# A values block in the free columns of a scores bank, other prices for changes of TensorE's form, and new ranks

## The chip, the cores and the metric

The kernel runs on one NeuronCore of a Trainium2 chip. The metric is device time in microseconds (us) of one execution; lower is better. Engine names below are those of the profile: PE (TensorE), DVE (VectorE), ACT (ScalarE), POOL (GpSimd) and SP (the queue that issues nearly all DMAs).

## The reference: attention, then a token and a channel mixer

```python
def _attn_ref(q, k, v, n_global, n_local):       # (4, 8, 768, 64), float32; n_global 8, n_local 96
    scores = scale * np.matmul(q, k.transpose(0, 1, 3, 2))
    is_global = pos[None, :] < int(n_global)
    is_local = (rel >= 0) & (rel < int(n_local))
    keep = is_global | is_local
    dist = np.where(is_global & ~is_local, float(n_local), np.abs(rel))
    scores = scores + (-slopes[:, None, None] * dist)[None]
    scores = np.where(keep, scores, -1e9)
    a = np.exp(scores - np.max(scores, axis=-1, keepdims=True))
    return np.matmul(a / (np.sum(a, axis=-1, keepdims=True) + 1e-09), v)

def _moe_ref(x, w_tok1, w_tok2, w_ch1, w_ch2):   # x: (4, 768, 512)
    h = np.maximum(x.transpose(0, 2, 1) @ w_tok1, 0.0) @ w_tok2
    u = x + h.transpose(0, 2, 1)
    return u + np.maximum(u @ w_ch1, 0.0) @ w_ch2
```

A row of the scores keeps 96 local keys and 8 global ones. The four weights are float64 in the test's input and reach the kernel as their raw bits.

## The kernel before

**The work.** Attention is cut into 48 units v = 0 to 47, twelve to each of the four batches (`pair`, L536). A unit is two heads by 256 queries, or two by 192 where it starts a sequence. On PE a unit has up to three blocks: **S** (its scores, two PSUM banks), **T** (transposes of the weights, only for units 0 to 19; later units are turned by DMA transposes between `split` and `join`), and **V** (weights times values, two banks). Between S and V stand `max` on DVE (it reads the scores out of PSUM, once for each of the two banks), `exp` on ACT, `sum`, `inv`, `norm`, the turning, and `back` or `join`. `put` copies V's output out of PSUM. After the twelve units of a batch come the token mixer (**N** transposes, **J** and **U** products), then the channel mixer (**F** and **g** products of 12 and 6 matmuls, 48 steps k), and for the last two of its six chunks a form with fewer products (**P**, **G**, **H**). The weights are decoded on ACT, DVE and POOL into pairs of float32r tiles while the first batch's attention runs (`bits`, `down`, `shift`, `sign`, `high`, `low`).

**TensorE's two forms.** S and V blocks use 64x64 quarters of the array (`form="quarters"`), everything else the whole 128x128 array. PE changes form each time one kind follows the other.

**What sets the order.** `Plan` (L125 to 258) holds every piece of work with its engine, cost, predecessors, rank and what it takes and gives (tile slots by name; PSUM banks as tuples such as `("sp", v, e)`). `record` runs a list schedule over these costs: whenever an engine is free it takes, among the pieces whose predecessors have ended and whose slots and banks are free, the one of the lowest rank, and on PE adds a price for a change of form. The order of each engine's instructions in the program is the order in which the schedule started them; at run time nothing is reordered, and only semaphores make an engine wait. `fast` is built on the result, with ranks from long tables at L1250 ff. (`PAIRS` for units, `CHANNEL` for the steps k, `MIXES`, `PRI` and so on).

**Banks.** PSUM has eight banks of 512 columns (`self.banks`). A scores block fills at most columns 0 to 383 of its two, a values block at most columns 0 to 127. `bank` (L335) makes a tile of the whole bank, `[P, 512]`. The semaphores are set by the tile framework from the accesses to each tile: an access waits for the accesses to the same tile by other engines that were recorded before it.

Of the kernel before, what the change touches and what calls it, by code (L numbers as in the profile page):

```python
# [26 lines left out]
P = 128  # L27
# [103 lines left out]
class Plan:  # L131
# [7 lines left out]
    def __init__(self, room, busy, engines):  # L139
        self.room, self.busy, self.engines = dict(room), busy, engines  # L140
        self.work, self.order = {}, []

        self.banks, self.held = list(range(8)), {}

    def add(self, name, engine, cost, run, after=(), rank=0.0, take=(), give=(), form=None, move=None):

        costs = engine if isinstance(engine, dict) else {engine: cost}
        self.work[name] = dict(name=name, costs=costs, run=run, after=sorted(set(after)), rank=rank, take=take, give=give,  # L150
                               form=form, move=move, choice=isinstance(engine, dict))

    def record(self):
# [17 lines left out]
        while events:  # L171
# [3 lines left out]
            if what == "end":  # L175
# [9 lines left out]
                for g in w["give"]:  # L185
                    if isinstance(g, tuple):
                        banks.append(self.held[g])
                    else:
                        room[g] += 1
# [4 lines left out]
            for e, names in ready.items():  # L194
# [20 lines left out]
                for names in ready.values():  # L215
                    if n in names:
                        names.remove(n)
                for t in w["take"]:
                    if isinstance(t, tuple):
# [42 lines left out]
PORT = 0.05, 0.105  # L262

# [33 lines left out]
class Fast:  # L297
# [161 lines left out]
    def pair(self, v):  # L459
# [97 lines left out]
        def values():  # L557
# [6 lines left out]
            g["op"] = [self.bank("op", v, i) for i in range(2)]  # L564
# [33 lines left out]
        for e in range(2):  # L598
            add(f"max{v}{e}", "dve", 0.54 if j else 0.48, lambda e=e: maxima(e), [f"S{v}"] + ([f"max{v}0"] if e else []),
                r - PRI['max'], wp if e == 0 else [], [("sp", v, e)])  # L600
            add(f"exp{v}{e}", "act", 0.88 if j else 0.83, lambda e=e: exps(e), [f"max{v}{e}"], r - PRI['exp'])
        add(f"sum{v}", *(("pool", 0.32) if FIRST <= v < PER else ("dve", 0.19)), sums, [f"exp{v}0", f"exp{v}1"], r - PRI["sum"])
        add(f"inv{v}", "dve", 0.1, inverses, [f"sum{v}"], r - PRI["sum"])
        for e in range(2):
            for i in range(2):
                p = 0.4 if j else (0.34, 0.56)[i]
                add(f"norm{v}{e}" + "_0" * (1 - i), dict(dve=0.27, pool=p) if v < FIRST or PER - 3 <= v < PER else dict(pool=p),
                    0, lambda en, e=e, i=i: norm(e, i, en), [f"norm{v}{e}_0" if i else f"inv{v}"], r - PRI["norm"])
        if not far:
            add(f"T{v}", "pe", 0.7, transposes, [f"norm{v}0", f"norm{v}1"], r - PRI["T"],  # L610
                [("tp", v, 0), ("tp", v, 1)])
            for e in range(2):
                add(f"back{v}{e}", dict(act=0.37, dve=0.46), 0, lambda en, e=e: back(e, en), [f"T{v}"],
                    r - PRI["back"], (), [("tp", v, e)])
            late, give = "back", wp + (["w"] if FIRST <= v < PER else [])
        else:
            for e in range(2):
                add(f"split{v}{e}", "dve", 0.48, lambda e=e: split(e), [f"norm{v}{e}"] + ([f"split{v}0"] if e else []), r - PRI["split"],
                    [] if e else ["mix", "mix"])
                add(f"turn{v}{e}", "sp", 1.28, lambda e=e: turned(e), [f"split{v}{e}"], -1000, move=TURNED)  # L620
                add(f"join{v}{e}", dict(act=0.93, dve=0.5), 0, lambda en, e=e: join(e, en), [f"turn{v}{e}"], r - PRI["join"], (), ["p"])
            late, give = "join", ["mix", "mix"]
        add(f"V{v}", "pe", 0.68 if j else 0.63, values, [f"{late}{v}0", f"{late}{v}1"] + ([f"V{PER * b + n}"] if j else []), r - PRI["V"],
            [("op", v, 0), ("op", v, 1)] + (["w"] if v < H // 2 else ["x"] if b and j == 0 else []), give, "quarters")
        for i in range(2):
            add(f"put{v}{i}", dict(act=0.16, dve=0.2), 0, lambda en, i=i: put(i, en), [f"V{v}"], r - PRI["put"], (), [("op", v, i)])


    def tokens(self, b):
# [72 lines left out]
        for s in range(NS):  # L702

            done = range(4 * (s // 2), 4 * (s // 2) + 4) if b == 0 else range(PER)
            add(f"N{b}{s}", "pe", 0.36, lambda s=s: nat(s),
# [23 lines left out]
    def channel(self, q):  # L729
# [47 lines left out]
        for f in range(NF):  # L777
# [3 lines left out]
                r - PRI["F"], [("hp", k)])  # L781
# [448 lines left out]
GROUP = 0  # L1230

TURNS = 0.1, 0.15

TURN = 20000.0
# [6 lines left out]
def rank(kind, *at):  # L1241
# [8 lines left out]
WEIGHTS = [-247287.64, -257459.66, -159802.66, 108347.25, 701320.36, 727424.03, 731700.59, -176028.47, -459899.46,  # L1250
    748998.43, -38407.14, 719519.09, -9340.29, 41643.28, 649601.75, -293679.97, -289307.55, -286192.76, -286154.59,
    599029.48, -288533.39, 576521.07, 574350.69, 619086.99, 690632.99, 615663.67, 350737.42, 602403.1, 350663.18,
    316597.46]
LOADS = [613978.2, 312816.36, 625641.67, 661111.23, 634176.56, 421225.21, 779927.82, 261887.11, 364054.34,
    634156.02, 779954.04, 379228.08, 364081.73, 749680.16, 379239.78, 3198492.43, 944262.45, 693856.62, 942541.96,
    944250.08, 364126.34, 262402.44, 3214978.83, 341772.37, 450658.52, 209511.38, 198960.32, 261800.84, 198940.7,
    3134618.01]
CHANNEL = [301486.65, 143282.3, 182530.41, 140462.62, 301502.01, 301530.53, -445928.27, 234721.3, -528799.29,
# [5 lines left out]
PAIRS = [-1226940.92, -1226961.87, -41406.37, -1244067.5, -73629.74, -39713.61, -3405.65, -570391.63, 16314.72,  # L1264
# [5 lines left out]
PRI = {'q': -136472.84, 'max': 36946.91, 'exp': 564950.24, 'sum': 384246.62, 'norm': -75198.73, 'T': 377235.02,  # L1270
    'back': -67350.38, 'split': -146960.38, 'join': 586267.28, 'V': 171989.17, 'put': 204986.15, 'F': -599619.09,
    'mix': 1187119.78, 'hid': 282479.97, 'send': 35006.69, 'high': 307017.91}
PRI2 = {'early': 38778.45, 'quad': -995662.53, 'mixed': -322415.37, 'second': -162956.33, 'step': -65687.24,
    'zmixed': 432393.84, 'hid': -315881.55, 'half': -273398.98, 'less': 233896.24, 'lstep': -298323.36, 'lstep2':
    -767970.86, 'late': -656740.22, 'evac': 433382.65, 'other': 235872.85}
OPERANDS = [-266472.19, -132411.79, -126401.41, 250209.8, 250863.15]
FORMS = [-101606.63, 339654.31, 605149.18, -102559.01, 567856.28, 867487.13, -122475.58, 490959.25, -205979.65,
    -96045.46, 547370.76, 423744.95]
PARK = [529904.06, -94029.49, 431875.51, 430818.8]
UNPARK = [464099.4, 464058.48]  # L1280
MIXES = [[211216.27, 227215.94, 235324.42, -655468.27, 276409.17, 413038.91, 275470.81, -587105.86, -579070.2,
# [255 lines left out]
```

## Time and profile before

| | |
|---|---|
| times of 3 runs | 579.27, 577.6, 579.19 us (median 579.19) |
| profiled execution | 577.9 us, its span 576.0 us |
| granted TensorE clock | 0.998 |
| PE busy | 558.8 us, 97% of the span |
| DVE, ACT, POOL busy | 413.0 (72%), 311.0 (54%), 291.0 us (51%) |
| PE's share of the chain that ended last | 85% |

The span runs from the first to the last instruction of the profiled execution; 1.9 us of its time lie around it. PE is busy nearly throughout, but over the first 56 us the slices of the profile's picture of busy time show it at 60 to 90%, and DVE and ACT at 80 to over 90%.

### The profile page before, as it was taken

Reading aid. Unit: us, or ns where it says so; the run is one execution under the profiler, and the core shown is the slowest. Engines: PE = TensorE matmul, PEld = TensorE weight load, DVE = VectorE, ACT = ScalarE, POOL = GpSimd, SP = SyncE. Lnnn points to the kernel's source line nnn. Section 1 sums busy time; section 2 is a strip of 40 time slices with the busy share of each in tenths; the row PEclk is TensorE's granted clock in tenths of the full one; section 3 lists DMA queues with packets and bytes.
Section 4 is the critical chain, followed back from the end, with each engine's and each line's share of the span. In section 5 each row is a group of like instructions: output and inputs, shape, how many; then the busy total and the mean of one; then the engine's idle time right before and its main releaser. Section 6 shows DMA issues by size and latency. Waiting matters only on the chain.

```text
span 576.0 us, 12239 instructions
## 1 busy us (share of the span) xinstructions
PE 558.8 (97%) x4402; PEld 454.5 (79%) x4402; DVE 413.0 (72%) x1029; ACT 311.0 (54%) x800; POOL 291.0 (51%) x405
## 2 busy tenths in 40 slices
PE   6889999999999999999999999999999999999996
PEld 5657887788888888888887887787788878888885
DVE  4998999976678888566436877657635964449885
ACT  3999988876645666333433723543533533337340
POOL 3796678531128777153305697714200233139982
PEclk9999999999999999999999999999999999999999
DMA  7948692877212879957320447998402173445013
GB/s 258 395 151 307 226 349 78 250 205 263 73 38 75 193 229 266 376 116 216 87 81 2 127 184 160 328 335 166 97 6 75 55 238 109 152 141 183 0 39 114
DMA packets 72083, 97.08 MB, mean 169 GB/s; under 512 B 47952, under 2 KB 51152, under 8 KB 72016
## 3 DMA queue, kind: packets, MB, share of 16 engines
q1 hardware_dynamic: 71728, 96.09, 53.7%
q8 instruction: 37, 0.61, 0.4%
q14 instruction: 30, 0.25, 0.1%
q10 hardware_dynamic: 288, 0.13, 0.1%
HBM read 63.18 MB, written 22.02 MB: 148 GB/s over the span
## 4 chain that ended last, share of the span: by engine, by line
PE 85%; DVE 4%; DMA 3%; ACT 3%; POOL 3%; issue 1%; ACTq 1%; SPq 0%; POOLq 0%
PE hp L288 31%; PE acc L288 22%; PE last L288 10%; PE pu L288 5%; PE op L288 5%; PE pj L288 5%; PE sp L288 4%; DVE pp L288 2%; DMA p<-r 2%; PE xtp L288 2%; PE tp L288 1%; DMA w<-wc 1%; POOL pp L288 1%; ACT pp L288 1%; DVE r L288 1%
## 5 line engine op out<-in xcount | busy, mean ns | idle before, releaser
L288 PE MATMUL hp<-uh,wc 128*128 128x512 f32 x432 | 140.9, 393 | 0.3 <-PE sp L288 0.3
L288 PE MATMUL acc<-hh,wc 128*128 128x512 f32 x384 | 120.7, 395 | 0.0
L288 POOL TENSOR_SCALAR p<-p,st 128x192 f32<-128x192 f32 (+1 forms) x132 | 80.2, 624 | 56.2 <-ACT p L288 30.6
L288 PEld LDWEIGHTS hp<-uh,wc 128*128 128x128 f32 x432 | 81.1, 188 | 20.1 <-ACT u L288 1.2
L288 PE MATMUL hp<-ul,wc 128*128 128x512 f32 x216 | 84.2, 390 | 0.0
L288 PEld LDWEIGHTS acc<-hh,wc 128*128 128x128 f32 x384 | 70.5, 188 | 16.4 <-issue 1.7
L288 PE MATMUL acc<-hl,wc 128*128 128x512 f32 x192 | 74.9, 390 | 0.0
L288 DVE COPY r<-p 128x768 uint16<-128x768 uint16 x82 | 54.1, 680 | 21.8 <-DMA p<-r 14.0
L288 ACT ACTIVATE p<-p,st 128x192 f32<-128x192 f32 (+1 forms) x132 | 57.4, 439 | 16.8 <-DVE st L288 16.8
L288 ACT ACTIVATE hh<-hp 128x512 fp32r<-128x512 f32 x48 | 28.6, 595 | 58.5 <-PE hp L288 38.4
L288 POOL TENSOR_TENSOR o<-uh,ul 128x512 f32<-128x512 f32 x16 | 22.8, 1435 | 66.1 <-DVE t L288 37.3
L288 DVE SCALAR_TENSOR_TENSOR hl<-hp,hh 128x512 fp32r<-128x512 f32 x48 | 33.0, 687 | 23.6 <-ACT hh L288 23.4
L288 DVE SCALAR_TENSOR_TENSOR t<-w,t 128x512 int32<-128x512 int32 x60 | 43.5, 729 | 6.1 <-ACT w L288 3.5
L288 PEld LDWEIGHTS hp<-ul,wc 128*128 128x128 f32 x216 | 40.6, 188 | 8.0
L288 POOL TENSOR_SCALAR e<-e,sc 128x256 f32<-128x256 f32 x37 | 24.1, 654 | 43.3 <-DMA e<-pk 31.2
L288 ACT COPY r<-p 128x768 uint16<-128x768 uint16 x30 | 31.6, 1066 | 21.6 <-DMA p<-r 12.4
L288 PEld LDWEIGHTS acc<-hl,wc 128*128 128x128 f32 x192 | 36.0, 188 | 7.7
L288 DVE CUSTOM_DVE_ANT_0 p<-sp,bias 128x192 f32<-128x192 f32 (+1 forms) x132 | 37.7, 343 | 5.3 <-PE sp L288 5.2
L288 POOL TENSOR_TENSOR hid<-hid 128x512 f32<-128x512 f32 x14 | 19.8, 1412 | 36.5 <-ACT hid L288 35.7
L288 PE MATMUL sp<-e 64*64 64x192 f32 (+1 forms) x624 | 32.4, 329 | 1.3 <-ACT e L288 0.8
L288 DVE TENSOR_TENSOR lent<-lent 128x256 f32<-128x256 f32 (+1 forms) x48 | 31.2, 683 | 1.9 <-ACT lent L288 1.8
L288 POOL TENSOR_SCALAR pp<-pp,st 128x192 f32<-128x192 f32 (+1 forms) x50 | 23.1, 476 | 10.2 <-DVE st L288 9.1
(184 smaller groups left out, 1196.8 us busy)
## 6 DMA issues: line engine op xcount, KB each, us to landing
e<-pk SPq DMA_DIRECT2D x24, 592.0 KB, 5.5
w<-wc SPq DMA_DIRECT2D x24, 512.0 KB, 6.7
sd<-lent SPq DMA_DIRECT2D x24, 512.0 KB, 3.5
e<-pk SPq DMA_DIRECT2D x14, 560.0 KB, 5.1
back<-wd SPq DMA_DIRECT2D x8, 768.0 KB, 7.3
lent<-sd SPq DMA_DIRECT2D x10, 512.0 KB, 3.8
sm<-sd SPq DMA_DIRECT2D x16, 256.0 KB, 3.3
unit<-pk SPq DMA_DIRECT2D x9, 384.0 KB, 6.4
```

The lines of the kernel that those rows point to most:

```text
L288: ins = getattr(self.engine, name)(*args, **kw)
```

## The change

- A pair of banks can hold one S block and one V block at a time. `join` puts a block into the latest pair that has none of its kind (`shared`), or takes two fresh banks; `leave` gives a bank back when both of its blocks are done with it. V writes columns 384 to 511 of its banks instead of 0 to 127; S stays where it was. In `bank` both blocks of a pair get **the same tile object**, so a shared bank goes by one name (that of the block that came first: an output `sp` of a V block, or `op` of an S block).
- The plan's price for a change of form goes from 0.1 and 0.15 us to 0.2 and 0.25 us in its time, its weight in the choice (`TURN`) from 20000 to 1209.99, and `GROUP`, which favours quarters when more of them are ready, from 0 to 20.92. `N` costs 0.44 us instead of 0.36.
- Four tables are added that shift the ranks of single units or steps (`SOFT`, `VALUES`, `PUTS`, `FIRSTS`), and all other ranks are new. The arithmetic is the same.

```diff
+    def shared(self, tokens):
+        if tokens[0][0] not in SLOTS:
+            return None
+        return next((p for p in reversed(self.pairs) if tokens[0][0] not in p["use"]), None)
+    def join(self, tokens):
+        p = self.shared(tokens)
+        if p is None:
+            p = dict(use=set(), banks=[self.banks.pop(0) for _ in tokens], left=[0, 0], tiles={})
+            self.pairs.append(p)
+        p["use"].add(tokens[0][0])
+        for t in tokens:
+            self.owner[t] = p
+            p["left"][t[2]] += 1
+    def leave(self, token):
+        p, e = self.owner[token], token[2]
+        p["left"][e] -= 1
+        if not p["left"][e]:
+            self.banks.append(p["banks"][e])
+            self.pairs = [x for x in self.pairs if x is not p]
...
-                    if len(some) <= len(banks) and all(room[t] >= w["take"].count(t) for t in w["take"] if t not in some):
+                    if (len(some) <= len(banks) or self.shared(some)) and all(room[t] >= w["take"].count(t) for t in w["take"] if t not in some):
...
+SLOTS = "sp", "op"
...
-        i = self.plan.held[(name, *key)]
-        return self.ps.tile([P, 512], F32, tag=f"b{i}", name=name)
+        pair = self.plan.owner.get((name, *key))
+        if pair is None:
+            i = self.plan.held[(name, *key)]
+            return self.ps.tile([P, 512], F32, tag=f"b{i}", name=name)
+        e = key[-1]
+        if e not in pair["tiles"]:
+            pair["tiles"][e] = self.ps.tile([P, 512], F32, tag=f"b{pair['banks'][e]}", name=name)
+        return pair["tiles"][e]
...
-            g["op"] = [self.bank("op", v, i) for i in range(2)]
+            g["op"] = [self.bank("op", v, i)[:, 384:] for i in range(2)]
...
-                r - PRI['max'], wp if e == 0 else [], [("sp", v, e)])
+                r - PRI['max'] + SOFT[v], wp if e == 0 else [], [("sp", v, e)])
...
-GROUP = 0
-TURNS = 0.1, 0.15
-TURN = 20000.0
+GROUP = 20.92
+TURNS = 0.2, 0.25
+TURN = 1209.99
...
+VALUES = [-648691.61, 62020.51, -661316.06, -60827.32, -467294.93, -879603.85, -879479.46, -66299.9, -373273.58,
...
```

Counted over the whole program, PE has 46 unbroken groups of quarter blocks before and 37 now; 12 of them stand ahead of the first J product in both. 26 of the V blocks share their banks with an S block. From the last J products of the fourth batch on, some 140 us before the end, all engines' orders are the same. Ahead of the first U product of the first batch PE had S of unit 21, T of unit 16 and V of units 16 and 17, which now stand behind it; nothing has come in their place.

Three places of the order follow. The first is DVE in the softmax of the first units, from the copy that completes unit 0's transposed weights (`back`), with what each row waits for. The two rows of `ISA` are the `max` of unit 1, one for each bank, the copies are unit 0's `put`, the last row is the first `max` of unit 3. Before, DVE has there:

```order
L288 COPY pp<-tp 128x384 [waits PE_49]
L288 ISA pp,st<-sp,bias 128x2x64 [waits PE_49]
...
L288 ISA pp,st<-sp,bias 128x2x64 [waits PE_49]
...
L288 COPY x<-op 128x128 [waits PE_49] x2
L288 ISA pp,st<-sp,bias 128x2x64 [waits PE_49]
```

Now DVE has there, with the shared bank under the name `sp`:

```order
L321 COPY pp<-tp 128x384 [waits PE_49]
L321 ISA pp,st<-sp,bias 128x2x64 [waits PE_49]
...
L321 ISA pp,st<-sp,bias 128x2x64 [waits PE_49]
...
L321 COPY x<-sp 128x128 x2
L321 ISA pp,st<-sp,bias 128x2x64 [waits PE_49]
```

The rows stand in the same order, but V of unit 0 now lies in the bank of unit 1's scores, and the copies out of it wait for nothing: the `max` rows ahead of them already wait for V's last matmul into that bank.

The second is PE a little later: V of unit 1 (`e_59` holds its values), with waits. Before, PE has there:

```order
L288 MATMUL op<-pp,e_59 64x128 [waits DVE_49]
L288 MATMUL op<-pp,e_59 64x128 [waits Activation_49]
L288 MATMUL op<-pp,e_59 64x128 [waits PE_49]
L288 MATMUL op<-pp,e_59 64x128 x3
L288 MATMUL op<-pp,e_59 64x64 x6
```

Now PE has there, again with the scores' bank as output:

```order
L321 MATMUL sp<-pp,e_59 64x128 [waits DVE_49]
L321 MATMUL sp<-pp,e_59 64x128 x5
L321 MATMUL sp<-pp,e_59 64x64 x6
```

Before, V waits for the two copies that bring its weights, one on DVE and one on ACT. Now it lies in the bank of unit 5's scores, and the one wait on DVE is for the last `max` of unit 5, which stands behind both copies on DVE.

The third is PE at the end of the fourth batch's attention (units 44 to 47; `e_58` to `e_61` hold a unit's loaded q, k and v; a row `64x192` is an S block, `64x128` with `64x64` a V block). Before, it is S and V blocks of 47 between those of 44 and 46:

```order
L288 MATMUL op<-r,e_58 64x128 x8
L288 MATMUL op<-r,e_58 64x64 x8
L288 MATMUL sp<-e_61 64x192 x8
L288 MATMUL op<-r,e_60 64x128 x8
L288 MATMUL op<-r,e_60 64x64 x8
```

Now the last group that holds an S block on PE is this one:

```order
L321 MATMUL sp<-e_60 64x192 x8
L321 MATMUL sp<-r,e_58 64x128 x8
L321 MATMUL sp<-r,e_58 64x64 x8
L321 MATMUL op<-r,e_61 64x128 x8
L321 MATMUL op<-r,e_61 64x64 x8
```

S of unit 46 has moved behind the products g of steps 42 and 43 and is now the last S block. V of unit 44 lies in its bank. Behind this group stand F of steps 44 and 45 and g of step 44, then V of units 45 and 46; before, S of unit 46 stood ahead of the second half of g of step 41, and the last S block was 47's.

## Rows read from the trace of the kernel before

**Rows 1.** The page: busy time of PE, and the chain that ended last.

```profile
PE 558.8 (97%) x4402; PEld 454.5 (79%) x4402; DVE 413.0 (72%) x1029; ACT 311.0 (54%) x800; POOL 291.0 (51%) x405
...
PE 85%; DVE 4%; DMA 3%; ACT 3%; POOL 3%; issue 1%; ACTq 1%; SPq 0%; POOLq 0%
```

**Rows 2.** Busy time by stretch: length, then PE, PEld, DVE, ACT, POOL; clock, DMA.

```profile
14.00:28.00 14.00, 12.42 (x252) 9.18 (x244) 13.14 (x82) 13.89 (x60) 10.49 (x30) 1.00 1.04 400
...
42.00:56.00 14.00, 12.72 (x281) 10.66 (x280) 11.65 (x47) 13.37 (x45) 9.67 (x17) 1.00 0.80 291
56.00:77.48 21.48, 21.36 (x317) 17.26 (x316) 20.97 (x56) 19.68 (x54) 14.14 (x23) 1.00 0.70 251
77.48:130.00 52.52, 52.52 (x425) 42.27 (x420) 46.46 (x118) 43.93 (x103) 32.11 (x33) 1.00 0.70 208
```

**Rows 3.** PE's timeline around a group of four quarter blocks: start, us, instructions.

```profile
255.31 0.39 PE L288 MATMUL acc<-hl,wc 128*128 128x512 f32 x1
255.63 0.88 PE L288 MATMUL sp<-e 64*64 64x192 f32 x16
256.33 0.85 PE L288 MATMUL op<-r,e 64*64 64x128 f32 x32
256.99 0.83 PE L288 MATMUL sp<-e 64*64 64x192 f32 x16
...
258.42 0.50 PE L288 MATMUL hp<-uh,wc 128*128 128x512 f32 x1
258.76 0.39 PE L288 MATMUL hp<-ul,wc 128*128 128x512 f32 x1
258.99 0.40 PE L288 MATMUL hp<-uh,wc 128*128 128x512 f32 x1
```

**Rows 4.** Timeline of PE, DVE and ACT in the first softmaxes.

```profile
13.78 0.29 DVE L288 CUSTOM_DVE_ANT_0 pp<-sp,bias 128x128 f32<-128x128 f32 x1 [0.73 <-PE sp L288]
...
14.45 0.22 PE L288 MATMUL op<-pp,e 64*64 64x64 f32 x1
...
19.16 0.76 PE L288 MATMUL op<-pp,e 64*64 64x128 f32 x18
...
19.92 0.82 PE L288 MATMUL sp<-keys,unit 64*64 64x192 f32 x14
...
20.39 0.08 DVE L288 DVE_READ_ACCUMULATOR2_ANT st<- 128x1 f32 x1
...
20.79 0.36 DVE L288 CUSTOM_DVE_ANT_0 pp<-sp,bias 128x192 f32<-128x192 f32 x1 [0.32 <-PE sp L288]
...
21.08 0.35 DVE L288 CUSTOM_DVE_ANT_0 pp<-sp,bias 128x192 f32<-128x192 f32 x1
...
22.43 0.46 ACT L288 ACTIVATE pp<-pp,st 128x192 f32<-128x192 f32 x1
```

**Rows 5.** Groups of ACT instructions from 12 to 76 us: busy us, mean ns.

```profile
L288 ACT COPY pp<-tp 128x384 f32<-128x384 f32 x15 | 7.0, 491 | 2.2 <-PE tp L288 2.2
...
L288 ACT ACTIVATE w<-w 128x512 f32<-128x512 f32 x8 | 5.5, 690 | 0.1
...
L288 ACT COPY x<-op 128x128 f32<-128x128 f32 x18 | 4.5, 293 | 0.3 <-PE op L288 0.2
...
L288 ACT CAST wc<-t 128x512 fp32r<-128x512 f32 x2 | 1.2, 622 | 0.7 <-DVE t L288 0.7
...
L288 ACT ACTIVATE unit<-unit,sc 128x256 f32<-128x256 f32 x1 | 0.5, 492 | 0.0
```

**Rows 6.** Timeline in the fourth batch: V of unit 37, S and last join of 47.

```profile
361.28 0.72 PE L288 MATMUL op<-r,e 64*64 64x128 f32 x16 [0.85 <-ACT r L288]
...
408.18 0.83 PE L288 MATMUL sp<-e 64*64 64x192 f32 x16
...
418.71 1.07 ACT L288 COPY r<-p 128x768 uint16<-128x768 uint16 x1
```

**Rows 7.** The page's DMA issues: the loads of a unit, KB, median us to landing.

```profile
e<-pk SPq DMA_DIRECT2D x24, 592.0 KB, 5.5
```

More of the change, by code (lines that the diff above doesn't have):

```diff
@@ L217, in record @@
                         names.remove(n)
+                some = [t for t in w["take"] if isinstance(t, tuple)]
+                if some and some[0][0] in SLOTS:
+                    self.join(some)
                 for t in w["take"]:
+                    if t in self.owner:
+                        continue
                     if isinstance(t, tuple):
@@ L599, in pair @@
             add(f"max{v}{e}", "dve", 0.54 if j else 0.48, lambda e=e: maxima(e), [f"S{v}"] + ([f"max{v}0"] if e else []),
-                r - PRI['max'], wp if e == 0 else [], [("sp", v, e)])
-            add(f"exp{v}{e}", "act", 0.88 if j else 0.83, lambda e=e: exps(e), [f"max{v}{e}"], r - PRI['exp'])
-        add(f"sum{v}", *(("pool", 0.32) if FIRST <= v < PER else ("dve", 0.19)), sums, [f"exp{v}0", f"exp{v}1"], r - PRI["sum"])
-        add(f"inv{v}", "dve", 0.1, inverses, [f"sum{v}"], r - PRI["sum"])
+                r - PRI['max'] + SOFT[v], wp if e == 0 else [], [("sp", v, e)])
+            add(f"exp{v}{e}", "act", 0.88 if j else 0.83, lambda e=e: exps(e), [f"max{v}{e}"], r - PRI['exp'] + SOFT[v])
+        add(f"sum{v}", *(("pool", 0.32) if FIRST <= v < PER else ("dve", 0.19)), sums, [f"exp{v}0", f"exp{v}1"], r - PRI["sum"] + SOFT[v])
+        add(f"inv{v}", "dve", 0.1, inverses, [f"sum{v}"], r - PRI["sum"] + SOFT[v])
         for e in range(2):
@@ L613, in pair @@
                 add(f"back{v}{e}", dict(act=0.37, dve=0.46), 0, lambda en, e=e: back(e, en), [f"T{v}"],
-                    r - PRI["back"], (), [("tp", v, e)])
+                    r - PRI["back"] + SOFT[v], (), [("tp", v, e)])
             late, give = "back", wp + (["w"] if FIRST <= v < PER else [])
@@ L704, in tokens @@
             done = range(4 * (s // 2), 4 * (s // 2) + 4) if b == 0 else range(PER)
-            add(f"N{b}{s}", "pe", 0.36, lambda s=s: nat(s),
+            add(f"N{b}{s}", "pe", 0.44, lambda s=s: nat(s),
                 [f"put{PER * b + v}{i}" for v in done for i in range(2)] + ([f"N{b}{s - 1}"] if s else []), r[s], [("xtp", b, s)])
@@ L1258 @@
-CHANNEL = [301486.65, 143282.3, 182530.41, 140462.62, 301502.01, 301530.53, -445928.27, 234721.3, -528799.29,
[5 rows of a table removed]
-PAIRS = [-1226940.92, -1226961.87, -41406.37, -1244067.5, -73629.74, -39713.61, -3405.65, -570391.63, 16314.72,
[5 rows of a table removed]
-PRI = {'q': -136472.84, 'max': 36946.91, 'exp': 564950.24, 'sum': 384246.62, 'norm': -75198.73, 'T': 377235.02,
-    'back': -67350.38, 'split': -146960.38, 'join': 586267.28, 'V': 171989.17, 'put': 204986.15, 'F': -599619.09,
-    'mix': 1187119.78, 'hid': 282479.97, 'send': 35006.69, 'high': 307017.91}
@@ L1273 @@
[L1273 to L1278, printed above, removed]
@@ new lines @@
+CHANNEL = [-2949169.64, -2510927.96, -3101480.77, -3123168.36, 576525.89, -2949169.27, -2947017.06, 955741.29,
[5 rows of a table added]
+PAIRS = [18126.21, -2488994.4, -75805.74, -191767.69, -142830.03, -2578991.51, -127250.42, -2457092.07, -126917.67,
[5 rows of a table added]
+PRI = {'q': -549637.56, 'max': 477943.31, 'exp': 1141466.61, 'sum': 881334.09, 'norm': 8677.43, 'T': 1141636.88,
+    'back': -188132.18, 'split': 60902.38, 'join': -528669.37, 'V': 277212.65, 'put': -528612.38, 'F': -545988.49,
+    'mix': 2305531.53, 'hid': 1665439.57, 'send': -356818.58, 'high': -259803.05}
@@ new lines @@
+PRI2 = {'early': -615955.21, 'quad': -726503.67, 'mixed': -600476.22, 'second': -241800.96, 'step': -625074.95,
+    'zmixed': -241788.36, 'hid': -656604.26, 'half': -326301.11, 'less': -241766.64, 'lstep': -414355.74, 'lstep2':
+    -884616.08, 'late': -864145.14, 'evac': -881205.61, 'other': -682843.25}
+OPERANDS = [-252627.04, -159434.83, -158488.82, -60757.83, -43455.52]
+FORMS = [1446332.6, 1432096.45, 1409418.05, 1423655.59, -119437.76, -116408.75, -286337.7, -119095.62, -94850.63,
+    -119433.56, -110237.18, -136161.96]
@@ L1288, in fast @@
+PARK = [65986.45, 64471.52, 19323.32, -648759.28]
+UNPARK = [-292592.4, 45309.19]
+MIXES = [[-912803.0, 384130.46, 270996.01, -912780.48, -683115.09, -655544.44, -798870.1, -569781.86, 320263.84,
[5 rows of a table added]
 @with_exitstack
```

39 lines of the change are left out of this document (21 added, 18 removed), and 49 rows, old and new, of tables (CHANNEL, FIRSTS, MIXES, PAIRS).

## The prediction

> **What bounds the kernel now.** I read the page first, then busy time by stretch, then the timeline at the places that the change touches. PE is busy for 558.8 of 576.0 us and has 85% of the chain that ended last [rows 1]. So the end is PE's start plus its work plus its idle time, and the change leaves the work alone. The stretches show where PE can wait. From 77.48 us, the start of the first U product, to 130 it is busy for 52.52 of 52.52 us. Before that, ACT is what is full: 13.89 of 14 us from 14 to 28, 13.37 of 14 from 42 to 56, with DVE at 13.14 and 11.65 and PE at 12.42 and 12.72 [rows 2]. So up to 77 us the pace is ACT's and DVE's, and PE idles between; after it, PE's own instructions count one for one. A saving on PE is worth its full price behind 77.48 us and little ahead of it.
>
> **The change of form.** The group of four quarter blocks at 255.63 gives its price. Two full matmuls follow each other by 258.99 - 258.76 = 0.23 us; from the last full one to the first quarter it is 255.63 - 255.31 = 0.32, so going in costs 0.09. A quarter block takes 256.99 - 256.33 = 0.66; the four take 258.42 - 255.63 = 2.79, or 0.15 more than 4 x 0.66. The first full matmul after them takes 0.34 instead of 0.23: another 0.11 [rows 3]. A trip into quarters and back costs 0.35 us. There were 46 and are 37. The 9 that go stand behind the first J product; 3 of them stand ahead of 77.48 us, 6 behind it. Behind: 6 x 0.35 = **-2.1 us**, in full. The 3 ahead of it (1.05 us) only let PE wait longer, if ACT and DVE still set the pace there.
>
> **The shared banks.** This is the part that the plan has no price for. A shared pair is one tile, so `max` of the S block waits for the V block in the same bank where V was recorded first, and V waits for `max` where that was first. The trace of before has no such case, since S and V never lay in one bank; its cost is bounded from both sides: nothing, where the later one would have come later anyway, and at most the whole of the other's work. Three cases lie early, where ACT is full.
> - Unit 1's first `max` starts at 13.78 now. V of unit 0 has its last matmul at 14.45 and ends at 14.67 [rows 4]. `max` moves behind it: 0.9 later, and with it the `exp` for which ACT stands idle there.
> - V of unit 1 starts at 19.16 and S of unit 6 is behind it on PE (19.92), whose `max` is at 20.79. Unit 5's last `max` ends at 20.39 + 0.08 = 20.47. V of unit 1 has to wait for that, itself 0.9 later: 21.37. Then S of unit 6 0.76 later at 22.13 and its `max` 0.87 after that at 23.0; its `exp`, at 22.43 now [rows 4], can start when the first half of `max` is through, some 0.3 later: 23.3. So here too ACT is **0.9 us late** in all (the first delay is in it). DVE's two `put` copies now stand between and wait for the same V.
> - Two `put` of unit 3 on ACT lie in the bank of unit 7's scores, ahead of unit 7's `exp`, and wait for both its `max`. `exp` could start after the first; the second comes two reductions later, 2 x (21.08 - 20.79) = **0.6 us** [rows 4].
>
> Is ACT's list ahead of the first U product shorter? At the `exp` of unit 6 it has left out two `back` and two `put` that it had done by then, 2 x 0.49 + 2 x 0.29 = 1.6 us. Up to the last J product's relu the new list has one `exp` less (two of 0.46, 0.9), six `put` less (1.8), one `high` less (0.6), but two `q` and one `down` more (1.0 + 0.7): 1.6 us less in all [rows 4, 5]. The two cancel, so the lateness of 1.5 us stays and the first U product starts **1.5 us later**, unless ACT's remaining idle time takes it up: 0.11 + 0.63 us in the two stretches shown and 1.8 from 56 to 77.48 [rows 2].
>
> **What PE has not done by then.** S of unit 21, T of unit 16 and V of units 16 and 17 now stand behind the first U product. At 0.66 us a block [rows 3] that is 4 x 0.66 = **+2.6 us** of work that PE did in its idle time and now does where it has none.
>
> **Late waits.** V of unit 37 waited 0.85 us for its join [rows 6]; two more F blocks now stand ahead of it: -0.85. At the end of the fourth batch, S of unit 47 started at 408.18 and its last join ended at 418.71 + 1.07 = 419.78, 11.6 us later [rows 6]. The last S is now unit 46's, with V of 44 in its bank, so its `max` waits 0.66 more: 12.3. PE has behind it V of 44 and 47, F of 44 and 45, g of 44 and V of 45: with S itself 4 x 0.66 and 36 matmuls of 0.23, and one trip, 2.6 + 8.3 + 0.35 = 11.2 us. V of 46 waits **1.1 us**, and N is behind it. S of 45 and 46 need loads that V of 41 and 42 release; a load lands after 5.5 us [rows 7] and `q` takes 0.5 [rows 5], 6.0 and some 0.3 for two semaphores, against 24 matmuls of 0.23 and a trip, 5.9: 0.3 each, **0.6**. In all +0.85.
>
> **The sum.** -2.1 + 1.5 + 2.6 + 0.85 = +2.9 us, against the execution's own 577.9: 580.8. That execution is 1.3 under the median of the three runs; two of the four times lie near 577.7 and two near 579.2, so I add half of it, 0.6: **581.4 us**.
>
> The Trainium skill, in PSUM — Partial Sum Buffer, section PSUM bank collisions raise a hardware error, says that engines must be kept apart by bank and group of 32 partitions, not by address: a V block in other columns of the bank that `max` reads would still collide. No run here shows such a pair. If engines could be let into one bank in different columns, the waits of 0.9, 0.6 and 0.66 would go, and by the sum above the time would be 2.2 us less, 579.2.
>
> **Rivals.**
> - *The trips come through in full and the early lateness is taken up.* For it: ACT has 2.5 us of idle time in the stretches named. Then the first U product comes earlier by as much as PE's list is shorter, and what is left is 9 x 0.35 = -3.15: 574.8, or 575.4 by the runs. Against it: DVE and ACT cannot run ahead of their lists, and these are no shorter where it counts.
> - *Early lateness is taken up in part, late waits stay out.* The first U product starts when it did or a little sooner (-1), +2.6 - 2.1 and half the late waits: 0 on balance, 578.5.
> - *Bank guards pile up.* 26 V blocks share; 6 of them are priced above or lie before the first J. If each of the other 20 delayed its softmax by the 0.66 of a block and a third of that reached PE, it would be +4.4 on the sum: 586. It decides from the point where joins arrive with less than 0.66 to spare. Against it: between S and V stand 10 to 16 us of products in most places.
> - *The change of form costs PE nothing to remove* (another cost takes the place of the drain): the 2.1 goes, 583.5. Against it: [rows 3] show the price on both sides of the group.
>
> **How the numbers follow.** The forecast of a slightly slower kernel has 0.38, the first rival 0.2, the second 0.3, the third and fourth 0.12 together. About 0.3% (1.7 us) is what a measurement of this kernel can tell from no change. Faster by more: the first rival, 0.2. Within: the second and the lower edge of the forecast, 0.33. Slower: the rest, 0.47. The forecast's own range is 579.5 to 583.5; the range for 8 in 10 reaches to the first rival and short of the third, 575.5 to 585.
>
> **What would show it.** Right: unit 1's first `max` near 14.7 and V of unit 1 near 21.3 with a wait on DVE; the first U product at 78 to 80 us; a wait of about 1 us at V of unit 46; some 0.35 us a trip, with 37 groups. Wrong: the first U product ahead of 76 us, or V of unit 1 starting by 20; then the guards are hidden and the first rival holds. If the U product comes in time and the end is still late, the loss is in waits behind 77 us that I have not named.

## The result and the profile after

After takes 584.11 us (median of 6 runs, 583.05 to 585.07); before took 579.2 beside it. The ratio is 1.0087, 95% interval 1.0069 to 1.0104: **4.9 us slower**. In a later session it was 1.0135 (1.0118 to 1.0153), so ratios from two sessions agree only to about half a per cent; of the small differences below, only those between kernels of one session are firm. The profiled execution of after is its longest, 585.07 us with a span of 583.2, against 577.9 and 576.0: 7.2 us apart.

(In the rows below L321, and L226 or L228 in the experiments, is the helper's line that records nearly every instruction, L288 before.) The page of after, busy time and chain, answers to [rows 1]:

```profile
PE 558.3 (96%) x4402; PEld 456.2 (78%) x4402; DVE 414.4 (71%) x1014; ACT 314.3 (54%) x809; POOL 294.7 (51%) x411
...
PE 28%; DMA 1%; DVE 0%; POOL 0%; issue 0%; ACT 0%; POOLq 0%
```

PE does the same 4402 matmuls in the same busy time; 24.9 us of the span are idle now, 17.2 before. (The chain could be followed over only some 30% of the span.) So the loss is waiting, and the stretches say where. Ahead of the first U product and from there to the fourth batch's N products, first before, then after (columns as in [rows 2]):

```profile
0.00:77.48 77.48, 67.30 (x1072) 52.65 (x1072) 65.87 (x279) 65.32 (x228) 51.87 (x131) 1.00 0.75 272
77.48:424.00 346.52, 344.90 (x2673) 281.33 (x2668) 247.08 (x627) 187.73 (x471) 173.97 (x230) 1.00 0.60 173
```

```profile
0.00:77.86 77.86, 63.96 (x986) 50.63 (x987) 65.01 (x276) 63.58 (x220) 44.56 (x121) 0.98 0.70 255
77.86:431.00 353.14, 347.41 (x2756) 284.66 (x2751) 249.15 (x615) 192.79 (x489) 185.58 (x246) 1.00 0.61 174
```

PE's idle time (the length less its busy time) goes from 10.2 to 13.9 us in the first stretch and from 1.6 to 5.7 in the second; the rest of the execution is the same. After's stretches that answer to [rows 2] are these (length, then PE, PEld, DVE, ACT, POOL; clock, DMA):

```profile
14.00:28.00 14.00, 9.61 (x157) 6.45 (x151) 11.06 (x66) 11.30 (x50) 6.37 (x19) 0.88 0.97 360
42.00:57.22 15.22, 12.74 (x255) 10.44 (x255) 14.90 (x55) 13.70 (x44) 9.98 (x23) 1.00 0.41 150
57.22:77.86 20.64, 20.29 (x272) 16.46 (x269) 19.49 (x65) 20.52 (x62) 11.03 (x19) 1.00 0.77 292
77.86:130.00 52.14, 51.09 (x438) 41.82 (x433) 47.34 (x113) 46.61 (x112) 39.78 (x45) 1.00 0.73 230
```

From 14 to 28 us PE does 157 matmuls where it did 252, and DVE, ACT and POOL are all less busy than before: everything waits for something, or runs at half clock (below). The first U product still starts at 77.86, only 0.4 later than before, because 986 matmuls stand ahead of it and not 1072: the four blocks that were moved behind it. Behind it, where PE waited for nothing before, it now idles 1.05 us by 130.

The rest of the second stretch, again first before, then after:

```profile
130.00:424.00 294.00, 292.38 (x2249) 239.07 (x2250) 200.62 (x510) 143.80 (x369) 141.86 (x197) 1.00 0.58 167
```

```profile
130.00:431.00 301.00, 296.32 (x2320) 242.84 (x2319) 201.80 (x502) 146.18 (x378) 145.80 (x202) 1.00 0.58 164
```

PE's idle time there goes from 1.62 to 4.68 us.

**The first softmaxes.** After's timeline answers to [rows 4]:

```profile
14.54 0.29 DVE L321 CUSTOM_DVE_ANT_0 pp<-sp,bias 128x128 f32<-128x128 f32 x1 [1.43 <-PE sp L321]
...
21.49 0.35 DVE L321 CUSTOM_DVE_ANT_0 pp<-sp,bias 128x192 f32<-128x192 f32 x1
...
21.91 0.72 PE L321 MATMUL sp<-pp,e 64*64 64x128 f32 x18 [0.76 <-DVE st L321]
...
22.85 0.36 DVE L321 CUSTOM_DVE_ANT_0 pp<-sp,bias 128x192 f32<-128x192 f32 x1 [1.00 <-PE sp L321]
...
24.33 0.45 ACT L321 ACTIVATE pp<-pp,st 128x192 f32<-128x192 f32 x1
```

Unit 1's first `max` starts at 14.54, behind V of unit 0 (before, it started at 13.78). V of unit 1 starts at 21.91 (19.16 before), and the row says what it waited for: DVE's `st`, the `max` of unit 5 in the bank that it writes. It is the first of that unit's two (its last reduction starts at 21.49), not the last, as the section on the change has it: the second, at 22.85, waits in turn for that V. Unit 6's `exp` starts at 24.33 (22.43 before).

Part of that is the clock. Two stretches, the one in which PE was busy 1.24 of 3.00 us (with columns as above), and the one in which the granted clock then was 0.50, that is 1.2 GHz:

```profile
14.00:17.00 3.00, 1.24 (x38) 0.89 (x32) 2.25 (x16) 2.12 (x10) 0.00 (x0) 1.00 1.04 415
...
17.56:20.97 3.41, 3.41 (x34) 2.00 (x26) 2.82 (x16) 2.98 (x14) 1.89 (x7) 0.50 1.01 394
```

S of unit 5 takes 1.51 us for its 16 matmuls there (from 19.64), where such a block takes 0.88 at the full clock. Before, the clock was 1.00 in all of this.

**Waits behind the first U product.** What PE waited for from 78 to 440 us in after (us in total, times, longest), the first three of six lines that sum to 5.7 us; before, the same table held three lines and 1.5 us:

```profile
PE sp L321 <- POOL e L321: 3.0, 4, 1.4
PE op L321 <- DVE r L321: 1.6, 1, 1.6
PE sp L321 <- DVE x L321: 0.4, 1, 0.4
...
```

S blocks (`sp`) wait for `q`, the scaling of the unit's queries, on POOL (`e`); V blocks wait for a `join` (`r`). The largest two on PE:

```profile
276.75 0.72 PE L321 MATMUL op<-r,e 64*64 64x128 f32 x21 [1.61 <-DVE r L321]
...
400.65 1.65 PE L321 MATMUL sp<-e 64*64 64x192 f32 x32 [1.37 <-POOL e L321]
```

Behind the second stands a chain that begins with shared banks. ACT's two `put` of unit 43 lie in the banks of unit 42's scores (the first row is DVE's, the end of a reduction of unit 42's first `max`):

```profile
394.13 0.08 DVE L321 DVE_READ_ACCUMULATOR2_ANT st<- 128x1 f32 x1
...
394.58 0.27 ACT L321 COPY x<-sp 128x128 f32<-128x128 f32 x1 [1.36 <-DVE st L321]
395.14 0.27 ACT L321 COPY x<-sp 128x128 f32<-128x128 f32 x1 [0.29 <-DVE st L321]
395.30 0.46 ACT L321 ACTIVATE p<-p,st 128x192 f32<-128x192 f32 x1
```

Each `put`, which only reads, waits for the `max` in its bank, which only reads; unit 42's `exp` stands behind both on ACT and starts at 395.30, 1.1 us after the first half of its `max` was through (394.13 + 0.08); unit 42's `norm` stands behind that on POOL, and `q` of unit 44 behind those. V of unit 43 had ended at 393.3.

### The profile page after: what moved, and what is told of

Read it like the earlier page. It is cut to its first block, busy times and chain, and to the rows that moved or that the text cites. A ratio compares the mean times of both kernels' runs of the same rounds, so it can differ in the third digit from the quotient of the medians.

```text
span 583.2 us, 12250 instructions
## 1 busy us (share of the span) xinstructions
PE 558.3 (96%) x4402; PEld 456.2 (78%) x4402; DVE 414.4 (71%) x1014; ACT 314.3 (54%) x809; POOL 294.7 (51%) x411
## 5 line engine op out<-in xcount | busy, mean ns | idle before, releaser
L321 PE MATMUL hp<-uh,wc 128*128 128x512 f32 x432 | 141.1, 393 | 0.2 <-ACT x L321 0.2
L321 PE MATMUL acc<-hh,wc 128*128 128x512 f32 x384 | 120.4, 394 | 0.3 <-POOL wc L321 0.3
L321 POOL TENSOR_SCALAR p<-p,st 128x192 f32<-128x192 f32 (+1 forms) x132 | 77.5, 603 | 71.5 <-ACT p L321 36.8
L321 PEld LDWEIGHTS hp<-uh,wc 128*128 128x128 f32 x432 | 81.0, 188 | 19.2 <-ACT u L321 1.2
L321 PE MATMUL hp<-ul,wc 128*128 128x512 f32 x216 | 84.2, 390 | 0.0
L321 PEld LDWEIGHTS acc<-hh,wc 128*128 128x128 f32 x384 | 70.9, 188 | 16.8 <-issue 1.7
L321 PE MATMUL acc<-hl,wc 128*128 128x512 f32 x192 | 75.0, 391 | 0.0
L321 DVE COPY r<-p 128x768 uint16<-128x768 uint16 x80 | 55.3, 714 | 27.6 <-DMA p<-r 15.2
L321 ACT ACTIVATE p<-p,st 128x192 f32<-128x192 f32 (+1 forms) x132 | 57.4, 439 | 8.3 <-DVE st L321 8.3
L321 ACT ACTIVATE hh<-hp 128x512 fp32r<-128x512 f32 x48 | 28.6, 595 | 56.2 <-PE hp L321 33.8
L321 DVE SCALAR_TENSOR_TENSOR hl<-hp,hh 128x512 fp32r<-128x512 f32 x48 | 32.9, 686 | 30.1 <-ACT hh L321 29.8
L321 DVE SCALAR_TENSOR_TENSOR t<-w,t 128x512 int32<-128x512 int32 x60 | 46.7, 785 | 4.2 <-ACT w L321 2.6
L321 POOL TENSOR_TENSOR o<-uh,ul 128x512 f32<-128x512 f32 x16 | 23.3, 1472 | 51.0 <-DVE t L321 35.1
L321 PEld LDWEIGHTS hp<-ul,wc 128*128 128x128 f32 x216 | 40.6, 188 | 8.0
L321 ACT COPY r<-p 128x768 uint16<-128x768 uint16 x32 | 34.0, 1070 | 17.7 <-DMA p<-r 17.7
L321 PEld LDWEIGHTS acc<-hl,wc 128*128 128x128 f32 x192 | 36.0, 188 | 8.4 <-DVE hl L321 0.8
L321 POOL TENSOR_TENSOR hid<-hid 128x512 f32<-128x512 f32 x14 | 19.7, 1410 | 36.4 <-ACT hid L321 35.6
L321 POOL TENSOR_SCALAR e<-e,sc 128x256 f32<-128x256 f32 x36 | 22.1, 617 | 25.8 <-DMA e<-pk 24.2
L321 POOL TENSOR_TENSOR lent<-lent 128x256 f32<-128x256 f32 (+1 forms) x29 | 28.0, 980 | 10.3 <-ACT lent L321 7.8
L321 POOL TENSOR_SCALAR pp<-pp,st 128x192 f32<-128x192 f32 (+1 forms) x50 | 22.3, 460 | 14.9 <-DVE st L321 13.8
L321 POOL TENSOR_TENSOR ul<-x,uh 128x256 fp32r<-128x256 f32 (+1 forms) x15 | 16.0, 1070 | 27.3 <-ACT uh L321 27.1
L321 DVE TENSOR_TENSOR lent<-lent 128x256 f32<-128x256 f32 (+1 forms) x43 | 28.6, 702 | 1.3 <-ACT lent L321 1.2
```

The source lines that it names most:

```text
L321: ins = getattr(self.engine, name)(*args, **kw)
```

## The theories

The kernel's own plan gives a yardstick. I took the order of each kernel, its plan's durations and the new prices, added for each access to a shared bank a wait for the earlier ones there, and computed when each piece would start. Without the added waits after's order ends at 561.9 us and before's at 566.1, so the plan did find 4.2 us. With them after's ends at 566.6: **the whole gain of the plan is the price of the waits that it leaves out**. That explains 0.5 of the 4.9 us; the chip takes 12 us beyond this replay for before (578.1 is the middle of its medians, 577.4 to 579.2) and 17.5 to 18.6 for after. Three theories for it:
1. Shared banks cost the time (1b: the low clock that follows from them).
2. The order of the change costs it, the banks do not.
3. The new prices do. At the old ones PE fell behind its own plan: the fourth batch's N was planned 407.9 us behind the first S block and came 417.5 behind it (423.7 - 6.2); the replay at the new prices says 416.6, so these fit the chip. While PE was late by up to 9.6 us, every other engine had that much room. A plan at prices that fit gives none of that room.

## The experiments

All but after_again and before_prices write the order of every engine out as a list (`ORDER`, piece:engine:banks) that `record` follows in place of its schedule:

```diff
+        for line in ORDER.split():
+            n, e, banks, join = (line + ":::").split(":")[:4]
...
+            if w["choice"]:
+                w["run"](self.engines[e])
+            else:
+                w["run"]()
...
+ORDER = """
```

"Beyond replay" is the median less the replay.

| run | groups | replay, us | median, us (before beside it) | ratio to before, 95% | beyond replay |
|---|---|---|---|---|---|
| before | 46 | 566.1 | 577.4 to 579.2 | 1 | 12 |
| after | 37 | 566.6 | 584.11 (579.2) | 1.0087 (1.0069 to 1.0104) | 17.5 |
| before_shared | 46 | 569.9 | 581.04 (578.07) | 1.0058 (1.0037 to 1.0080) | 11.1 |
| after_fewer | 37 | 564.7 | 581.12 (578.07) | 1.0058 (1.0036 to 1.0079) | 16.4 |
| after_filled | 37 | as after | 582.43 (578.07) | 1.0081 (1.0052 to 1.0109) | 15.8 |
| after_again | 37 | 566.6 | 585.22 (577.44) | 1.0135 (1.0118 to 1.0153) | 18.6 |
| plan_unshared | 36 | 565.3 | 581.47 (577.44) | 1.0082 (1.0057 to 1.0107) | 16.2 |
| plan_guards | 37 | 562.1 | 579.44 (577.44) | 1.0032 (1.0015 to 1.0048) | 17.3 |
| cheap_unshared | 44 | 565.2 | 578.26 (578.02) | 1.0001 (0.9983 to 1.0018) | 13.1 |
| cheap_guards | 42 | 564.7 | 577.76 (578.02) | 0.9996 (0.9972 to 1.0019) | 13.1 |
| before_prices | 48 | 572.3 | 586.41 (578.2) | 1.0161 (1.0128 to 1.0194) | 14.1 |
| plan_margin | 42 | 566.2 | 576.23 (578.2) | 0.9969 (0.9946 to 0.9992) | 10.0 |

The three experiments from before_shared to after_filled were made on one chip, all from after_again on another; on which chip the first runs of before and after were made is not on record.

**before_shared.** Only bank numbers change; `:+` puts a V block into the tile of the S block there. The first pair, and what follows from it for the next blocks:

```diff
-V0:pe:67
-S3:pe:01
-S4:pe:23
+V0:pe:45:+
+S3:pe:67
+S4:pe:01
```

> Every engine's instructions in the order of the kernel before, none moved; only the banks differ: 18 values blocks now lie in the free columns of a bank of a scores block, as in the change (S1 with V0, S5 with V1, S14 with V3, S2 with V4, S8 with V5 and 13 later ones). Theory 1, the accesses to a shared bank are run one after another and that costs time which the plan leaves out: replaying this order with the plan's durations and one wait more for each access to a shared bank puts the join product J00 2.2 us later, the first U product 3.7 and the end 4.3 us, so 579.2 + 4.3 = 583.5 (582 to 586). Theory 2, the waits on shared banks are hidden and the order of the change costs the time: 579.2, within 0.6.

1.0058, that is 3.4 us (2.1 to 4.6): theory 1, and not theory 2. Not an instruction moved, so the waits on shared banks cost time, some nine tenths of the 3.8 us that the replay at the new prices gives (566.1 to 569.9; the 4.3 of the expectation is at the old prices). The profiled execution was an outlier of 585.5 us, so its rows are not used.

**after_fewer.** The edit is of the same kind, the other way:

```diff
-V0:pe:45:+
+V0:pe:67
```

> Every engine's instructions in the order of the kernel after, none moved; 11 values blocks share a bank in place of 26, wherever two other banks were free at the planned time (the pairs S1 with V0, S5 with V1 and S7 with V3 are gone). Theory 1 (waits on shared banks): the same replay gives 1.9 us less than after, and 1 to 1.5 more if the low clock at 17.6 to 21 us goes with the waits of the first units: 584.1 - 1.9 = 582.2 (580.5 to 583). Theory 2 (the order costs it): 584.1, within 0.6.

1.0058 against 1.0087 in the first session: 1.7 us less by the ratios, where the replay has 1.9, but the intervals overlap and the sessions differ. It supports theory 1 and doesn't prove it alone. What stays is more than shared banks explain: 16.4 beyond the replay.

**after_filled.**

```diff
+            if n == "S3":
+                self.fill()
...
+        t = self.ps.tile([P, 512], F32, tag="b0", name="idle")
+        for _ in range(16):
+            self.pe.transpose(t[:, :P], self.ident, self.ident)
```

> The kernel after with 16 transposes of the identity added behind S3, into a bank that is free then, so that TensorE is busy in the 1.9 us before S4 in which it waited; S4 should start at the same time. Theory 1b, the low clock at 17.6 to 21 us (granted 0.5 to 0.64, after TensorE was busy 1.24 of 3 us) costs 0.8 to 1.5 us of the first units and stays to the end: the granted clock is 1.00 there and the time 584.1 - 1.2 = 582.9 (582.4 to 583.4). Rival: the low clock falls into waits for other engines and costs nothing, 584.1 within 0.4.

PE in that run, with the fill (`idle`) and V of unit 1:

```profile
15.39 1.97 PE L228 MATMUL idle<-ident 128*128 128x128 f32 x16
17.46 0.88 PE L228 MATMUL sp<-keys,unit 64*64 64x192 f32 x16
...
21.12 0.72 PE L228 MATMUL sp<-pp,e 64*64 64x128 f32 x18 [1.16 <-DVE st L228]
```

The clock was 1.00 from 15.1 us to 31, and 0.50 in the 3.4 us ahead of that, where in after it had risen at 14.1; V of unit 1 came 0.8 sooner than in after, still behind `max`, and the end came at 1.0081. The fill cost S4 0.4 us. Inconclusive: as ratios theory 1b asked for 1.0064 and the rival for 1.0085, and the interval (1.0052 to 1.0109) holds both; a gain of more than 2 us lies outside it. In the second profiled execution of after (after_again's) the low stretch lay at 26.7 to 30.1, and in plan_guards a second one began at 200.2, so it doesn't belong to one place of the order. Theory 1b is not the bulk.

**after_again, plan_unshared, plan_guards.** For the latter two an order was searched anew (random changes of ranks, judged by the plan's end) and written into `ORDER`. For plan_guards the plan also held the rule that it lacks, that a piece touching a shared bank starts when the earlier ones there have ended. Of its list, with V of 41 in the bank of S of 47:

```diff
+put420:dve put421:act load46:sp join411:dve S47:pe:27 max440:dve V41:pe:27:+ max441:dve exp440:act F42:pe:3 max470:dve
```

> The kernel after, unchanged, on the chip and beside the runs of the next two, so that they are compared with it there: 1.0087 times before as at first (1.007 to 1.0105).

> The rules and prices of the change (0.2 and 0.25 for a change of form, 0.44 for N) with no sharing of banks, and an order found anew by the same kind of search over ranks; its plan ends at 565.3 us, where that of after ends at 561.9 and that of before, with the changes of form at the same prices, near 568.2. The profiled execution of before took 9.7 us more than its plan so priced, that of after 23.2. Theory 1 (only the waits on shared banks are missing from the plan): 565.3 + 9.7 = 575.0 in such an execution, 0.995 times before. Theory 3 (an order fitted this closely to the plan has its S and V blocks only just in time, and loses some 8 us to waits of any kind even without shared banks): 583, 1.009 times before.

> As the one before, but with sharing where fewer than two banks are free, and with the waits on shared banks in the plan (an item that touches a shared bank starts when the earlier ones on it have ended); 13 values blocks share, the plan ends at 562.1. Theory 1: 562.1 + 9.7 = 571.8, 0.9895 times before. Theory 3: 562.1 + 18 = 580, 1.004 times before (1.000 to 1.008).

(568.2 for before adds every price in full; replayed, some fall into waits: 566.1, used from here on.) Theory 1 alone is refuted: with no shared bank at all plan_unshared is 1.0082, 4.7 us slower than before, from a plan that ends sooner. Theory 3's numbers were 1.009 and 1.004. Both theories hold a part: blind sharing (after_again) is 0.5% slower than no sharing, and sharing that the plan knows of 0.5% faster, as far as three orders from separate searches can say that.

**cheap_unshared, cheap_guards.** The same searches, at the old prices; the kernels are again lists, the edit is in the plan that was searched:

```diff
-TURNS = 0.2, 0.25
+TURNS = 0.1, 0.15
...
-            add(f"N{b}{s}", "pe", 0.44, lambda s=s: nat(s),
+            add(f"N{b}{s}", "pe", 0.36, lambda s=s: nat(s),
```

> As plan_unshared (no sharing, an order found anew), but the search saw the old prices of a change of form and of N (0.1 and 0.15, 0.36). Replayed at the new prices its order ends at 565.2 us, that of plan_unshared at 565.3, that of before at 566.1. Theory 3 (the old prices made TensorE late against its plan, by some 9 us at the end, and so gave every other engine that much room; at the new prices the S and V blocks are met just in time and waits of all kinds show): as much beyond the replay as before, 565.2 + 12 = 577.2, 0.998 times before (0.994 to 1.002). Rival (any order fresh from a search loses as much, at either price; that of before was picked on the chip): as plan_unshared, 581.3, 1.008 times before.

> As plan_guards (sharing where fewer than two banks are free, its waits in the plan), but the search saw the old prices. Replayed at the new ones its order ends at 564.7 us, that of plan_guards at 562.1. Theory 3: 564.7 + 12 = 576.7, 0.997 times before (0.993 to 1.001). Rival: 564.7 + 17, 581.7, 1.0065 times before.

1.0001 and 0.9996, both in theory 3's range; the rival's 1.008 and 1.0065 lie far outside the intervals. plan_unshared and cheap_unshared were searched alike but for the prices, and end at 565.3 and 565.2 in the replay; the same chip puts 0.8% between them, 4.7 us. So the price that the search saw matters. The other pair says the same: plan_guards is 2.6 us ahead of cheap_guards in the replay and 2 us behind it on the chip. Three things stay open:
- One order was searched for each case, so how far two orders of one search differ is not known.
- The orders searched at the new prices also have fewer groups (36 and 37, against 42 to 46). That fewer and longer groups lose the time, and not the missing room, is a rival that no run excludes. before_prices below, with 48 groups and 14.1 beyond its replay, speaks against it but lies in between.
- The traces don't show the 4.7 us: the profiled execution of plan_unshared is the fastest of its six (579.68), that of cheap_unshared the slowest of its twelve (579.61).

The room itself can be counted. A replay like the table's (its ends lie 0.1 to 2.1 us later) leaves less than half a microsecond to 2 to 4 of the S and V blocks behind the first U product in before, before_shared, cheap_unshared and plan_margin, to 6 in before_prices, and to 10 to 14 in after, after_fewer, plan_unshared and plan_guards. That is what theory 3 asks for, but for cheap_guards, which has 10 and lost no more than cheap_unshared.

**before_prices.** The same two edits turned round, in before itself:

> The kernel before with its own ranks and no sharing, and only the prices of the change (0.2 and 0.25 for a change of form, 0.44 for N): the plan falls out anew, with 48 groups of scores and values blocks in place of 46, and ends at 572.3 us, where the order of before, replayed at these prices, ends at 566.1. The ranks were found for the old prices, so a loss is expected on any theory, and its size tells how far the plan can be trusted: the 6.2 us of the plan and what before takes beyond it, 1.0107 times before (1.007 to 1.015).

1.0161, worse than any other and above what was expected (1.007 to 1.015): 14.1 beyond its replay, not 12. The prices alone, under ranks made for others, do not carry over.

**plan_margin.** Room put in openly, in the plan that was searched: 0.05 us more in `LATENCY` of PE, DVE, ACT and POOL, and

```diff
-TURNS = 0.2, 0.25
+TURNS = 0.15, 0.2
...
-TURNED = 1.15, 1.5
+TURNED = 1.15, 1.8
```

> As plan_guards, but the search saw 0.15 and 0.2 for a change of form, 0.44 for N, 0.05 us more from the end of one engine's item to the start of another's, and 0.3 more for a transposing transfer to land: room for the other engines put in openly, half way between the two prices. Replayed at the new prices without that room its order ends at 566.2 us, that of before at 566.1, that of plan_guards at 562.1. Theory 3 (what an order loses beyond its replay hangs on the room that its plan leaves): 12 beyond the replay, 578.2, 1.000 times before (0.996 to 1.003). Rival (orders fresh from a search at other prices than the old lose 16 to 17): 582.7, 1.008.

0.9969 (0.9946 to 0.9992), 1.8 us faster than before and the only one that beats both kernels; theory 3 asked for 0.996 to 1.003, its rival for 1.008. Ten of its V blocks share a bank. The prices, the latencies and the landing time were changed together, so which of them did it is open. The stretch from 130 to 427 us (the fourth batch's N starts at 422.6), to be laid beside the two above:

```profile
130.00:427.00 297.00, 296.99 (x2276) 244.02 (x2275) 200.26 (x504) 138.48 (x365) 150.44 (x209) 1.00 0.58 162
```

PE is idle for 0.01 us of 297, and its list of waits from 78 to 440 us is empty.

## Where after's waits lie

With the plan at hand, each wait of after can be held against the room that its plan left there: the planned start less the planned end of what it needs, a semaphore's time taken off. Behind the first U product 15 of after's 59 S and V blocks have less than 0.5 us, 6 of before's 56 by its own plan, against which PE ran late. Nine of the 15 are among the blocks that lost most (PE's time from the block before, less bare matmuls). In the two profiled executions of after these are:

| block | needs | room in the plan | lost | lost, second |
|---|---|---|---|---|
| g of step 5 | `low` on POOL | 0.18 | 0.57 | 0.23 |
| S20 | `q` on POOL | 0.46 | 0.95 | 0.95 |
| V27 | `join` | 0.08 | 0.77 | 0.81 |
| V35 | `join` | 0.31 | 2.00 | 0.14 |
| S44 | `q` on POOL | 0.36 | 1.53 | 1.36 |
| S45 | `q` on POOL | 0.14 | 0.58 | 0.56 |
| S46 | `q` on POOL | 0.44 | 0.63 | 0.39 |
| V47 | `join` | 0.20 | 0.61 | 0.61 |
| S40 | `q` on POOL | 0.18 | some 0.4 | some 0.5 |
| V46 | `join` | 0.17 | 0.33 | 0.32 |

All had under half a microsecond. They sum to 8.4 us and 5.9; a part of that before loses too (V of 37 waited 0.85 there, [rows 6]). By idle time, PE loses 5.7 and 3.4 us between the first U product and the fourth batch's N, against 1.6 in before: 4.1 and 1.8 us more (the second is the shortest of its four executions), of the 5.5 to 6.6 that after takes beyond before's 12. That these waits are the bulk of it is argued from their sizes and from plan_margin, where they are gone. Which of the small errors of the plan each one met was followed up for S44 (above) and V35 (below) alone, and where plan_unshared loses its time was not found.

## Why the prediction was right, and where not

581.4 was forecast, 575.5 to 585 as the range, slower as the likeliest; 584.11 lies near its upper end. It lies inside by the width of the range and not by the sum, which put 2.9 us between the executions where 7.2 were measured. Step by step:
- **The change of form, -2.1:** the count (27 to 21 groups behind the first U product) holds, and so does the price in after, both ways. PE's timeline at V of 45 and 46 shows the same 0.32 us from the last full matmul to the first quarter as [rows 3] (427.85 - 427.53), and behind them 0.57 for two full ones (430.13 - 429.56), that is 0.34 + 0.23. What the trips saved in the end was not measured by itself:

```profile
427.53 0.39 PE L321 MATMUL acc<-hl,wc 128*128 128x512 f32 x1
427.85 1.78 PE L321 MATMUL op<-r,e 64*64 64x128 f32 x64
429.56 0.73 PE L321 MATMUL acc<-hh,wc 128*128 128x512 f32 x2
430.13 0.39 PE L321 MATMUL acc<-hl,wc 128*128 128x512 f32 x1
```

- **The first shared banks, +1.5:** the waits came where they were said to come: unit 1's `max` at 14.54 (14.7 forecast), V of unit 1 at 21.91 behind DVE (21.37), unit 6's `exp` at 24.33 (23.3). Their reason was right only in the first case. V of unit 1 waited for the first `max` of unit 5 and not for its last, the second `max` waited for V, which was not forecast, and the half clock lengthened S of unit 5 by 0.6 us, so that 21.91 lies near 21.37 is partly luck. The two `put` of unit 3 held ACT up for 0.29 us and not 0.6 (the second starts at 31.18 with that wait). What it all does to the first U product was wrong: +0.4, and 77.86 where 78 to 80 was asked for. I had ACT's shorter list and two waits cancel by a count of instructions, but the new order reaches that product sooner by nearly as much as the waits make it late; in the replay the waits on shared banks put it 2.8 us later, and on the chip the order takes back nearly all of that.
- **Work moved behind it, +2.6:** as counted.
- **Late waits, +0.85: this is the step that failed.** V of 37 no longer waits (-0.85, right):

```profile
369.88 0.39 PE L321 MATMUL hp<-uh,wc 128*128 128x512 f32 x1
370.20 0.90 PE L321 MATMUL op<-r,e 64*64 64x128 f32 x24
```

  V of 46 lost 0.33 and not 1.1. S of 45 and 46 lost 0.6 each, where 0.3 each by the loads was forecast (by its own terms, 6.0 + 0.3 - 5.9, it was 0.4; the 0.3 for two semaphores stands in no row). For S of 46 the reason holds, its `q` on POOL waited for the load:

```profile
416.30 0.48 POOL L321 TENSOR_SCALAR e<-e,sc 128x256 f32<-128x256 f32 x1 [0.21 <-DMA e<-pk]
```

  The rest was not named: S20, V27, V35, S40, S44. From the first U product to the end, after takes 505.3 us (583.2 - 77.86) and before 498.5 (576.0 - 77.48), 6.8 more. Of that 2.6 is the work that was moved; 4.2 stays in spite of the 2.1 that the trips should save. So late waits cost some 6.3 us and not 0.85.
- **The rivals:** "bank guards pile up" (586) asked for joins with less than 0.66 us to spare and was set aside because 10 to 16 us of products stand between S and V. That was the wrong measure: the unit's own chain fills that time, and the plan leaves 0.1 to 0.5. The sentence that held was the last of "what would show it": the U product in time, the end late, waits behind it that had not been named.
- **Bank guards.** The Trainium skill, in PSUM — Partial Sum Buffer, section PSUM bank collisions raise a hardware error, asks for guards by bank, not by address. The rows agree as far as the program goes: its semaphores make V of unit 1 and the `put` of unit 43 wait for the `max` that reads other columns of their bank; in before_shared 18 such pairs cost 3.4 us (2.1 to 4.6). Whether the chip would stand it without the waits was not tried.
- That the new prices themselves could cost time was in none of my cases. They fit the chip, and orders searched with them still came out slower than orders searched with the old ones.

## What to carry to other kernels

When a list schedule is fitted to a cost table, a cost that is too low on the engine that bounds is room for all the others. If it is corrected, the room has to come back under its own name (latency, landing time): without it the orders here lost more than the better prices gained. plan_margin did this half way, with prices between the old and the new. When two uses come to share a buffer, write the waits that sharing brings into the schedule first: here, in the replay, they ate the whole planned gain. And judge "there is plenty between them" by what the plan leaves at the consumer, not by the work between the two ends.

## What the runs showed of the hardware

The last `join` of unit 35 waited 2.60 us for its transposing transfer in one execution of after and 0.72 in the other, at the same place of the same program; first the one, then the other:

```profile
272.90 0.61 DVE L321 COPY r<-p 128x768 uint16<-128x768 uint16 x1 [0.73 <-DMA p<-r]
276.10 0.60 DVE L321 COPY r<-p 128x768 uint16<-128x768 uint16 x1 [2.60 <-DMA p<-r]
```

```profile
273.11 0.61 DVE L321 COPY r<-p 128x768 uint16<-128x768 uint16 x1 [0.74 <-DMA p<-r]
274.44 0.61 DVE L321 COPY r<-p 128x768 uint16<-128x768 uint16 x1 [0.72 <-DMA p<-r]
```

The other three transfers of this kind from 266 to 278 us landed in 2.7 to 2.8 us; that one took 4.7. (Elsewhere in this execution they take longer: from 378 to 392 us, with loads of 768 KB on the same queue, the median is 6.6.) A piece of code (16 KB) was fetched at 273.8 and 273.9 us in the two, so that alone does not tell them apart, and the cause stays open. It accounts for some 2 us of the profiled execution, and a plan without 2 us to spare there pays it.

The granted clock fell to 0.50 at different places in two executions of one program: at 17.56 us in the first (above), and in the second in these two stretches, PE busy 1.78 of 3.41 us and then at half clock:

```profile
23.30:26.71 3.41, 1.78 (x29) 1.04 (x22) 3.41 (x23) 3.32 (x16) 2.79 (x10) 1.00 1.04 399
26.71:30.12 3.41, 3.41 (x34) 2.33 (x30) 2.10 (x10) 3.38 (x12) 3.24 (x9) 0.50 0.78 298
```

Its first U product came at 78.33 us, 0.5 from the other's.
